# A routed expert kernel: the nest of wide tiles behind the sure tiles, and row scatters that are no longer paced

## The chip, the cores and the metric

The kernel runs on one core of a Trainium2 chip. That core has five engines that run side by side and wait for one another through semaphores: TensorE (PE in the profile; its weight loads are listed as PEld), VectorE (DVE), ScalarE (ACT), GpSimd (POOL) and SyncE (SP). SP issues most loads; GpSimd issues the indirect transfers, whose row addresses come from a table in on-chip memory. All transfers share 16 DMA engines. The metric is the device time of one execution in microseconds; lower is better.

## The reference

Two blocks follow each other. The first is chunked attention: 4 batches, 8 heads, 768 tokens, 64 values a head. Each chunk of 32 queries sees 8 memory keys and the keys from 16 before to 8 behind its chunk.

```python
scores = scale * np.matmul(q_c, k_full.transpose(0, 1, 3, 2))
a = np.exp(scores - np.max(scores, axis=-1, keepdims=True))
a = a / (np.sum(a, axis=-1, keepdims=True) + 1e-09)
out[:, :, c_start:c_end] = np.matmul(a, v_full)
```

The heads are joined to rows of 512 values, 3072 rows in all. The second block sends each row through one of 8 experts, two matrices of 512x1024 and 1024x512. A row may keep the expert of the row before it, so the choice is a recurrence along the sequence.

```python
fresh_e = int(np.argmax(logits[b, s]))
e = fresh_e if s == 0 or local_gate[b, s] < 0.5 else prev_e
h = np.maximum(x[b, s] @ w1[e], 0.0)
out[b, s] = p[e] * (h @ w2[e])      # p: softmax of the logits
```

Everything is in 32-bit floats.

## The kernel before

**Attention.** The 3072 rows are worked in 32 blocks of 96 rows, eight a batch (the loop at L748). Per block PE makes scores (`s_ps`), ACT their exponentials, PE the values (`o_ps`), DVE divides by the sum and writes the block into `x`, and PE turns it (`xt_ps`). PE's order is that of the program text: L654 wraps every matmul and transpose so that the scheduler keeps its place. Other engines' instructions are ordered by a scheduler.

**Routing.** Four blocks make a half of a batch. For each half, a chain planned for later blocks (`plan_at`, L686 to L697) makes logits, picks, the recurrence over the sequence (two scans on DVE), and a row address for each row. Then `route_rows` (L458) computes the addresses and the scale of each row, and `scatter` (L474) sends the rows of one block to `x_dram`, a DRAM buffer with a region per expert: one indirect transfer of 96 rows on GpSimd. `route_rows` sends the first block of the half; the other three follow one attention block later each (L696). `behind` (L396, used in L479) makes each scatter also wait for `paced[0]`, the DVE instruction that last wrote a block of `x` when the scatter was recorded. For the last batch the scatters stand between the matmuls of the first two expert tiles (`MOVE_2` to `MOVE_6` and `MOVES` in `between`, L884 to L890).

**The early plan.** After two of the four batches (`FORE`), a plan is made of five early tiles (`EARLY`): 128 rows of one expert each, out of rows already there. `gathered` (L610) fetches the rows of a tile from `x_dram` by an indirect transfer. It has to wait until the scatters of the batches in question have landed. The five early gathers are planned one an attention block (L741, `early_gathered`, L712). `first_turned` (L731) turns the first tile on PE while attention's last blocks still run.

**Expert tiles.** A tile is 128 rows through one expert: `hidden` (L785) does 64 short matmuls into `h_ps`, with a ReLU on ACT, `rows_turned` (L715) turns the next tile's rows through the single PSUM buffer `g_ps`, and `product` (L801) does 16 long matmuls into `y_ps`; ACT scales, and GpSimd stores the rows to `out` by an indirect transfer (L809). The weights of a tile are eight loads of 512 KB on SP (L636 for `w1`, L639 for `w2`), into pool `wa` (two buffers) or `wb` (one).

Twelve tiles are always run (`SURE`). A late plan (L899) counts what else is left. In front of the ninth sure tile (`BRANCH`, i = 8) a nest of conditions runs further tiles as counted (`maybe_tiles`, L853); in this input eight of them run. In front of the tenth a second nest runs wide tiles (`wide_tiles`, L867): 128 rows plus 64 more of the same expert, so the hidden matmuls have 192 columns, and the last 64 rows have a product of their own (`unit_product`, L815, stored in L829). Three of eight wide tiles run. The first wide tile's weights are loaded into `wa`, the others' into `wb`. Its rows are gathered during tiles i = 6 and 7 and turned in tile i = 8 (`wide_turned`). The last three sure tiles come behind the nest.

A condition that fails jumps over the rest of its nest to a short block that brings the semaphores to where the skipped instructions would have left them, and for that it waits for the engine's own work; these instructions are listed as `_compat.py:109`. After tile i = 9 GpSimd executes one `drain` (L950). At the end all engines read a count (`kept`, L93), and jump over a general version of the kernel that this input doesn't need (L94).

Of the kernel before, what the change touches and what calls it, by code (L numbers as in the profile page):

```python
# [9 lines left out]
I32 = mybir.dt.int32  # L10
ACT = mybir.ActivationFunctionType
ALU = mybir.AluOpType
# [220 lines left out]
def everything(ctx, tc, q, k, v, w_gate, w_local, w1, w2, x_dram, out, ident, back, kept_i):  # L233
# [117 lines left out]
    def values(pt, vt, n, x):  # L351
        for u in range(2):
            o_ps = ops.tile([QB, HP, VW], F32, name="o_ps", tag=f"o_ps{u}")
            for a in range(HP):
                nc.tensor.matmul(o_ps[:, a], lhsT=pt[:, u, a], rhs=vt[:, 2 * a + u], start=True, stop=True)
            rinv = rinvs[:, n, u]
            nc.vector.reciprocal(rinv, o_ps[:, :, DH:VW])
            paced[0] = nc.vector.tensor_tensor(  # L358
                x[:, 0:D].rearrange("p (a u d) -> p u a d", u=2, d=DH)[:, u], o_ps[:, :, 0:DH],
                rinv.to_broadcast([QB, HP, DH]), op=ALU.mult).ins  # L360

    def turned(x, xt):
        xt_ps = xps.tile([P, DK, QB], F32, name="xt_ps", tag="xps")
# [26 lines left out]


    scatters = {b: [] for b in range(B)}

    paced = [None]

    def behind(ins, name):  # L396
        tc.add_manual_dep(ins, name, mybir.DependencyInfo(
            mybir.DependencyClass.Sync, mybir.DependencyReason.DATA), reason="rows written, or one a block")

    def begin_route():  # L400
        return {n: sm.tile([QB, NQB, w], F32, name=n, bufs=2) for n, w in (("lt", E + 1), ("ex", E))}
# [56 lines left out]
    def route_rows(r, b, half, x):  # L458

        j = HALF * half  # L460
        rank, tot, ex = r["rank"], r["tot"], r["ex"][:, j:j + HALF]
        r_ps = xps.tile([QB, HALF, E], F32, name="r_ps", tag="xps")
        for n in range(HALF):
            nc.tensor.transpose(r_ps[:, n], rank[:, QB * (j + n):QB * (j + n) + QB], identity=ident[:E, :E])
        row = sm.tile([QB, HALF], I32, name="row", bufs=2)
        nc.vector.tensor_reduce(row, r_ps, axis=AX.X, op=ALU.max)
        nc.vector.scalar_tensor_tensor(ex, r_ps, 0.0, ex, ALU.is_gt, ALU.mult)
        prob = sm.tile([QB, HALF, 1], F32, name="prob")
        nc.vector.tensor_reduce(prob, ex, axis=AX.X, op=ALU.add)
        nc.vector.tensor_tensor(x[0:QB, j:j + HALF, D:D + 1], prob, tot, op=ALU.mult)  # L470
        r["row"] = row
        scatter(r, b, j, 0)

    def scatter(r, b, j, n):  # L474
        x = xs[b]
        ins = nc.gpsimd.indirect_dma_start(  # L476
            out=x_dram[:, :], out_offset=bass.IndirectOffsetOnAxis(ap=r["row"][:, n:n + 1], axis=0),
            in_=x[0:QB, j + n].bitcast(I32), in_offset=None).ins
        behind(ins, paced[0].name)  # L479

        tc.declare_no_dep(ins, group="scatters", query=mybir.DependencyQuery.ANY_SYNC, reason="rows are unique")
        tc.add_to_no_dep_group("scatters", ins)
        scatters[b].append(ins)

# [123 lines left out]
    def gathered(tiles, i, after, xs=None):  # L610
        _, rows, _ = tiles
        if xs is None:
            xs = gx.tile([P, XW], F32, name="xs")
        ins = nc.gpsimd.indirect_dma_start(
            out=xs.bitcast(I32), out_offset=None, in_=x_dram[:, :],
            in_offset=bass.IndirectOffsetOnAxis(ap=rows[:, i:i + 1], axis=0)).ins
        for a in after:
            for s in scatters[a]:
                behind(ins, s.name)
        tc.add_to_no_dep_group("scatters", ins)  # L620
        return xs

# [21 lines left out]
    def weights(tiles, i, pool):  # L644
        w, pieces = weights_begun(tiles, i, pool)
        for p in pieces:
            p()
        return w
# [34 lines left out]
    def plan_at(at, step, f, *args):  # L683
        at.setdefault(step, []).append(lambda: f(*args))

    for g in range(NB // HALF):  # L686
        b, half = divmod(g, 2)
        n = HALF * g + HALF + 2
        plan_at(first, n, half_logits, g)
        plan_at(after, n, half_turned, g)  # L690
        plan_at(after, n + 1, lambda b=b, half=half: route_picks(routes[b], half))
        plan_at(after, n + 2, lambda b=b, half=half: route_experts(routes[b], half))
        plan_at(after, n + 3, lambda b=b, half=half: route_ranks(routes[b], b, half))
        plan_at(after, n + 3, lambda b=b, half=half: route_places(routes[b], half))
        plan_at(after, n + 4, rows, b, half)
        for j in range(1, HALF):  # L696
            plan_at(after, n + 4 + j, lambda b=b, half=half, j=j: scatter(routes[b], b, HALF * half, j))  # L697

    early = {}

# [8 lines left out]
        early["w"], pieces = zip(*(weights_begun(early["tiles"], i, wa) for i in range(2)))  # L709
        early["pieces"] = [p for ps in pieces for p in ps]  # L710

    def early_gathered(i):  # L712
        early.setdefault("xs", []).append(gathered(early["tiles"], i, range(FORE)))

    def rows_turned(tiles, i, xs, ps=None, xt=None):  # L715
        _, _, past = tiles
# [21 lines left out]
    n = NQB * FORE + HALF + 2  # L738
    plan_at(after, n, plan_begun)
    plan_at(after, n + 1, planned)  # L740
    for i in range(EARLY):  # L741
        plan_at(after, n + 4 + i, early_gathered, i)
    plan_at(after, NB - 3, first_turned)
    for n in range(NB - 8, NB):
        plan_at(after, n, some_pieces, 1)
# [94 lines left out]
    def wide_gathered(j):  # L840
        for t, xs in zip((wide, unit), wide_slots(j)):
            gathered(t, j, range(B), xs)
# [10 lines left out]
    def maybe_tiles(ctx, n_tiles):  # L853
        last = NTILE - SURE - 1
        for j in range(NTILE - SURE):
# [7 lines left out]
                maybe_turned(j + 1)  # L863
            product(ht, w2_sb, rest[:, j % RING], late[2][:, i:i + 1])

    @with_exitstack
    def wide_tiles(ctx, n_wide, w):  # L867
        for j in range(E):
            ctx.enter_context(tc.If(n_wide > j))
            if j + 2 < E:  # L870
                wide_gathered(j + 2)
            w1_sb, w2_sb = weights(wide, j, wb) if j else w
            ht = hidden(wide_xt[j % 2], w1_sb, rows=MORE, ht=wide_ht[j % 2])
            if j + 1 < E:
                wide_turned(j + 1)
            xs, xs_unit = wide_slots(j)
            product(ht, w2_sb, xs, wide[2][:, j:j + 1])
            unit_product(ht, w2_sb, xs_unit, unit[2][:, j:j + 1], wide_y[j % 2])
# [2 lines left out]
    pools = (wa, wa, wb)  # L881

    after.setdefault(NB, []).insert(0, lambda: turn(NB - 1))
    left = [f for n in range(NB, NB + HALF + 6) for f in first.pop(n, []) + after.pop(n, [])]  # L884
    (TURN, MOVE_2, EXPERTS_0, MOVE_3, RANKS_0, PLACES_0, LOGITS, ROWS_0, TURNED, MOVE_4, PICKS, MOVE_5, EXPERTS_1,
     MOVE_6, RANKS_1, PLACES_1, ROWS_1, *MOVES) = left
    between = {0: {0: [MOVE_2], 1: [TURN], 2: [MOVE_3], 3: [LOGITS], 4: [EXPERTS_0], 5: [TURNED],
                   6: [RANKS_0, PLACES_0, PICKS]},
               1: {0: [ROWS_0], 1: [EXPERTS_1, MOVE_4], 2: [RANKS_1, PLACES_1, MOVE_5], 3: [MOVE_6],
                   7: [ROWS_1, *MOVES]}}  # L890

    late = None
    tile_xs, tile_w, done = early["xs"], list(early["w"]), early["done"]
# [1 line left out]
    for i in range(SURE):  # L895
# [16 lines left out]
        if i == BRANCH:  # L912
            _, (n_tiles, n_wide) = nc.values_load_multi_w_load_instructions(
                n_i, min_val=0, max_val=NTILE, skip_runtime_bounds_check_because="counts of tiles")
            nc.tensor.matmul, nc.tensor.transpose = pinned(matmul), pinned(transpose)
            maybe_tiles(n_tiles)

            wide_w = weights(wide, 0, wa)
            tile_w.append(weights(late, i + 1 - EARLY, wa))
        if i == BRANCH + 1:  # L920
            wide_tiles(n_wide, wide_w)
            nc.tensor.matmul, nc.tensor.transpose = matmul, transpose
        if late is not None:
            while len(tile_xs) < min(i + 4, SURE):
                tile_xs.append(gathered(late, len(tile_xs) - EARLY, range(B)))
            while len(tile_w) < min(i + 3, SURE) and (len(tile_w) <= BRANCH or i > BRANCH):
                tile_w.append(weights(late, len(tile_w) - EARLY, pools[len(tile_w) % 3]))
        if BRANCH - 4 <= i < BRANCH - 2:
            with tc.issue_after(stored):
                maybe_gathered(i - (BRANCH - 4))  # L930
        if BRANCH - 2 <= i < BRANCH:
            with tc.issue_after(stored):
                wide_gathered(i - (BRANCH - 2))
        w1_sb, w2_sb = tile_w[i]
        ht = hidden(xt, w1_sb, between.get(i, {}))
        if i == 0:
# [2 lines left out]
            nc.vector.tensor_copy(kept_i, k_ps)  # L939
        if i + 1 < SURE:  # L940
            tiles, at_i = (early["tiles"], i + 1) if i + 1 < EARLY else (late, i + 1 - EARLY)
            ahead = rows_turned(tiles, at_i, tile_xs[i + 1], xt=held_xt[0] if BRANCH <= i + 1 <= BRANCH + 1 else None)
        if i + 1 == BRANCH:
            maybe_turned(0)
        if i == BRANCH:
            wide_turned(0)
        stored = product(ht, w2_sb, tile_xs[i], past)
        if i == SURE - 3:

            tc.keep_in_program_order(nc.gpsimd.drain())  # L950
        xt, past = ahead
        if i == 0:
            nc.tensor.matmul, nc.tensor.transpose = matmul, transpose


# [38 lines left out]
```

## Time and profile before

| | us |
|---|---|
| median of 3 runs | 516.69 |
| the runs | 516.51, 516.69, 518.14 |
| the profiled execution's own time | 518.14 |
| its span in the profile | 516.2 |
| PE busy | 493.4 (96%) |
| POOL busy | 101.0 (20%) |
| attention until the first expert matmul | 0 to 123.3 |
| first nest (eight tiles) ends on PE | 376.0 |
| second nest (three wide tiles) on PE | 393.5 to 459.7 |
| PE's last matmul ends | 510.1 |

The profile shows one execution. A line of a timeline gives start, duration, engine, source line, operation, output and inputs, the count, and in brackets the idle time in front of it with what ended it. Names that end in q are an engine's own queue: branches, semaphore steps and drains, which do not count as busy. A granted clock below 1.00 means that PE's clock was held back; the digits of the PEclk row are tenths of the full clock in 40 equal slices. An indirect transfer's duration on POOL is the making of its descriptors; it lands some microseconds later.

### The profile page before, as it was taken

How to read it: one execution, taken by the hardware profiler on the slowest of the kernel's cores; microseconds unless marked ns; L12 is line 12 of the kernel's file. 1: busy time of each engine (PE TensorE's matmuls, PEld its weight loads, DVE VectorE, ACT ScalarE, POOL GpSimd, SP SyncE). 2: the span in 40 equal slices, each digit the busy share in tenths (PEclk: the TensorE clock that was granted, in tenths of full speed). 3: DMA queues.
4: the chain of work that ended last, by engine and by line, in shares of the span. 5: the costliest groups of instructions: out<-in, count | busy, mean ns of one | idle time of the engine just before them, and what ended most of it. 6: DMA issues, size and time to landing. Idle time of an engine off the chain costs nothing. (4 is left out here: it accounts for less than half of the span.)

```text
span 516.2 us, 9234 instructions
## 1 busy us (share of the span) xinstructions
PE 493.4 (96%) x3474; PEld 378.8 (73%) x3474; DVE 109.5 (21%) x437; ACT 110.9 (21%) x234; POOL 101.0 (20%) x151
## 2 busy tenths in 40 slices
PE   8999999949999999999999999999989999979995
PEld 5988888839678777777777777777777695838772
DVE  2456668634356000001000000000010000000000
ACT  4555555511111111010111111010111111100100
POOL 3002332335043121122111111001102030210000
PEclk9999999966999999999999999999999999997999
DMA  8988888996999999999989999895179925778000
GB/s 299 366 287 245 264 282 247 374 408 208 413 299 356 396 316 360 344 372 354 335 327 325 315 325 336 318 337 204 38 277 414 359 69 187 291 275 324 22 22 24
DMA packets 49377, 146.01 MB, mean 283 GB/s; under 512 B 7258, under 2 KB 11358, under 8 KB 49312
## 3 DMA queue, kind: packets, MB, share of 16 engines
q1 hardware_dynamic: 42240, 123.38, 67.0%
q0 software_dynamic: 6784, 21.30, 11.3%
q8 instruction: 34, 0.56, 0.4%
q10 hardware_dynamic: 288, 0.52, 0.3%
q14 instruction: 31, 0.25, 0.1%
HBM read 132.57 MB, written 13.00 MB: 282 GB/s over the span
## 5 line engine op out<-in xcount | busy, mean ns | idle before, releaser
L654 PEld LDWEIGHTS h_ps<-held_xt,w_sb 128*128 128x128 f32 x704 | 81.6, 194 | 6.6 <-issue 4.9
L654 PE MATMUL h_ps<-held_xt,w_sb 128*128 128x128 f32 x704 | 82.3, 277 | 0.9 <-ACTq _compat.py:109 0.9
L654 PE MATMUL y_ps<-w_sb,ht 128*128 128x512 f32 x176 | 77.5, 593 | 0.0
L809 POOL DMA_INDIRECT out_dram<-y,to x24 | 24.2, 1006 | 257.0 <-ACT y L808 244.4
L804 PE MATMUL y_ps<-w_sb,ht 128*128 128x512 f32 x160 | 70.5, 592 | 0.0
L793 PEld LDWEIGHTS h_ps<-gxt,w_sb 128*128 128x128 f32 x576 | 65.8, 192 | 3.9 <-issue 3.8
L793 PE MATMUL h_ps<-gxt,w_sb 128*128 128x128 f32 x576 | 66.3, 275 | 0.0
L654 PEld LDWEIGHTS y_ps<-w_sb,ht 128*128 128x128 f32 x176 | 32.6, 190 | 36.9 <-issue 36.4
L804 PEld LDWEIGHTS y_ps<-w_sb,ht 128*128 128x128 f32 x160 | 29.5, 190 | 33.0 <-issue 32.8
L796 ACT ACTIVATE ht<-h_ps 128x512 f32<-128x512 f32 x42 | 25.1, 597 | 126.6 <-PE h_ps L793 65.9
L654 PE MATMUL o_ps<-vt,pt 128*96 128x65 f32 x512 | 51.7, 256 | 0.1
L654 PEld LDWEIGHTS o_ps<-vt,pt 128*96 128x96 f32 x512 | 48.7, 172 | 2.9 <-DVE base L446 1.2
L476 POOL DMA_INDIRECT x_dram<-x,row x32 | 31.4, 983 | 82.0 <-DVE x L470 48.9
L722 DVE COPY held_xt<-g_ps 128x512 f32<-128x512 f32 x13 | 9.0, 692 | 158.6 <-PE g_ps L654 144.1
L654 PEld LDWEIGHTS s_ps<-qt,kt 64*128 64x128 f32 x512 | 29.9, 188 | 6.3 <-issue 2.9
L654 PE MATMUL s_ps<-qt,kt 64*128 64x96 f32 x512 | 32.7, 277 | 0.4 <-ACT pt L348 0.4
L654 PEld LDWEIGHTS h_ps<-x,w_sb 128*128 128x128 f32 x192 | 31.2, 190 | 1.2 <-issue 1.2
L654 PE MATMUL h_ps<-x,w_sb 128*128 128x192 f32 x192 | 31.9, 327 | 0.0
L348 ACT ACTIVATE pt<-s_ps,mask_mid 128x256 f32<-128x256 f32 x72 | 28.0, 481 | 7.1 <-PE s_ps L654 6.5
L358 DVE TENSOR_TENSOR x<-o_ps,rinvs 96x256 f32<-96x256 f32 x64 | 26.3, 418 | 1.2
L808 ACT ACTIVATE y<-y_ps,x 128x512 f32<-128x512 f32 x12 | 8.2, 687 | 83.1 <-PE y_ps L654 76.3
L808 ACT ACTIVATE y<-y_ps,xs 128x512 f32<-128x512 f32 x12 | 8.2, 687 | 83.1 <-PE y_ps L804 61.8
(207 smaller groups left out, 353.6 us busy)
## 6 DMA issues: line engine op xcount, KB each, us to landing
w_sb<-in_w_dram SPq DMA_DIRECT2D x192, 512.0 KB, 7.4
vt<-in_v_dram SPq DMA_DIRECT2D x32, 260.0 KB, 4.2
kt<-in_k_dram SPq DMA_DIRECT2D x30, 256.0 KB, 4.6
qt<-in_q_dram SPq DMA_DIRECT2D x32, 192.0 KB, 4.2
kt<-in_k_dram ACTq DMA_DIRECT2D x2, 256.0 KB, 3.6
x_dram<-x,row POOLq DMA_INDIRECT x32, 6.3
out_dram<-y,to POOLq DMA_INDIRECT x24, 7.2
x<-x_dram,rows_late POOLq DMA_INDIRECT x11, 7.2
```

The costliest lines, as they stand in the source:

```text
L348: nc.scalar.activation(pt[:, :, :, c], st[:, :, :, c], ACT.Exp, bias=m[:, g:g + 1], scale=SCALE)
L358: paced[0] = nc.vector.tensor_tensor(x[:, 0:D].rearrange("p (a u d) -> p u a d", u=2, d=DH)[:, u], o_ps[:, :, 0:DH], rinv.to_broadcast([QB ...
L476: ins = nc.gpsimd.indirect_dma_start(out=x_dram[:, :], out_offset=bass.IndirectOffsetOnAxis(ap=r["row"][:, n:n + 1], axis=0), in_=x[0:QB, ...
L654: return lambda *a, **k: tc.keep_in_program_order(f(*a, **k))
L722: nc.vector.tensor_copy(xt[:, :, 0:P], g_ps)
L793: nc.tensor.matmul(h_ps[:, m], lhsT=w1_sb[:, kk, P * (g + m):P * (g + m) + P], rhs=xt[:, kk, 0:rows], start=(kk == 0), stop=(kk == DK - 1))
L796: nc.scalar.activation(ht[:, g:g + many], h_ps, ACT.Relu)
L804: nc.tensor.matmul(y_ps, lhsT=ht[:, m, 0:P], rhs=w2_sb[:, m], start=(m == 0), stop=(m == FK - 1))
L808: nc.scalar.activation(y, y_ps, ACT.Copy, scale=xs[:, D:D + 1])
L809: return nc.gpsimd.indirect_dma_start(out=out, out_offset=bass.IndirectOffsetOnAxis(ap=to, axis=0), in_=y, in_offset=None, bounds_check=NT ...
```

## The change

Two things change together.

First, the pacing goes. `route_rows` sends the four scatters of a half one behind the other, they no longer wait for `paced[0]`, and the five early gathers are issued together, at the block after the plan.

Second, the wide nest moves behind all twelve sure tiles, to the kernel's end. Its first weights go to `wb`, the others' to `wa` with its two buffers; the late sure tiles from the tenth on take `wa`. The first wide gathers are issued during tiles i = 9 and 10, and the first wide rows are turned in tile i = 11. The drain after tile i = 9 goes; in its place GpSimd drains in front of the nest and once in each wide tile, behind the gathers that the tile issues.

```diff
+        for n in range(HALF):
+            ins = nc.gpsimd.indirect_dma_start(
+                out=x_dram[:, :], out_offset=bass.IndirectOffsetOnAxis(ap=row[:, n:n + 1], axis=0),
+                in_=x[0:QB, j + n].bitcast(I32), in_offset=None).ins
...
-        scatter(r, b, j, 0)
-
-    def scatter(r, b, j, n):
...
-        behind(ins, paced[0].name)
...
-        for j in range(1, HALF):
-            plan_at(after, n + 4 + j, lambda b=b, half=half, j=j: scatter(routes[b], b, HALF * half, j))
...
-    def early_gathered(i):
-        early.setdefault("xs", []).append(gathered(early["tiles"], i, range(FORE)))
+    def early_gathered():
+        early["xs"] = [gathered(early["tiles"], i, range(FORE)) for i in range(EARLY)]
...
-    for i in range(EARLY):
-        plan_at(after, n + 4 + i, early_gathered, i)
+    plan_at(after, n + 2, early_gathered)
...
+    def released():
+
+        tc.keep_in_program_order(nc.gpsimd.drain())
...
             if j + 2 < E:
                 wide_gathered(j + 2)
-            w1_sb, w2_sb = weights(wide, j, wb) if j else w
+            released()
+            w1_sb, w2_sb = weights(wide, j, wa) if j else w
...
-            wide_w = weights(wide, 0, wa)
-            tile_w.append(weights(late, i + 1 - EARLY, wa))
-        if i == BRANCH + 1:
-            wide_tiles(n_wide, wide_w)
-            nc.tensor.matmul, nc.tensor.transpose = matmul, transpose
...
-            while len(tile_w) < min(i + 3, SURE) and (len(tile_w) <= BRANCH or i > BRANCH):
-                tile_w.append(weights(late, len(tile_w) - EARLY, pools[len(tile_w) % 3]))
+            while len(tile_w) < min(i + 3, SURE) and (len(tile_w) <= BRANCH or i >= BRANCH):
+                tile_w.append(weights(late, len(tile_w) - EARLY, wa if i >= BRANCH else pools[len(tile_w) % 3]))
+        if i == SURE - 1:
+            wide_w = weights(wide, 0, wb)
...
-        if BRANCH - 2 <= i < BRANCH:
+        if SURE - 3 <= i < SURE - 1:
             with tc.issue_after(stored):
-                wide_gathered(i - (BRANCH - 2))
+                wide_gathered(i - (SURE - 3))
...
-        if i == BRANCH:
+        if i + 1 == SURE:
             wide_turned(0)
...
-        if i == SURE - 3:
-
-            tc.keep_in_program_order(nc.gpsimd.drain())
...
+    released()
+    wide_tiles(n_wide, wide_w)
+    nc.tensor.matmul, nc.tensor.transpose = matmul, transpose
```

## The prediction

> **What bounds the kernel now.** I read the page's slices first: TensorE (PE) is busy in all but two places, so a change can only save time where PE stands idle or runs slow.
>
> ```profile
> PE   8999999949999999999999999999989999979995
> PEclk9999999966999999999999999999999999997999
> ```
>
> Slice 9 (103 to 116 us) is a hole, with a clock of 0.6 around it; slice 37 (464 to 477 us) follows a smaller one. PE's timeline shows the first, and the table of stretches its clock (last three columns: granted clock, DMA share, GB/s).
>
> ```profile
> 105.33 0.50 PE L654 MATMUL xt_ps<-ident,x 96*128 96x96 f32 x4
> 112.79 1.08 PE L654 MATMUL g_ps<-ident,xs 128*128 128x128 f32 x4 [6.96 <-DMA xs<-x_dram,rows_early]
> 123.31 3.00 PE L654 MATMUL h_ps<-held_xt,w_sb 128*128 128x128 f32 x16
> 126.14 0.49 PE L654 MATMUL xt_ps<-ident,x 96*128 96x96 f32 x4
> ...
> 115.00:120.00 5.00, 4.84 (x32) 4.26 (x29) 1.74 (x7) 0.96 (x2) 2.30 (x2) 0.50 0.84 306
> 120.00:125.00 5.00, 5.00 (x30) 5.00 (x29) 3.14 (x21) 0.60 (x2) 2.36 (x5) 0.50 0.31 76
> ```
>
> PE waits 6.96 us for the first gather of tile rows, then works at half clock until about 125.4 us. GpSimd's timeline (POOL) says why the gather is late:
>
> ```profile
> 98.44 0.92 POOL L476 DMA_INDIRECT x_dram<-x,row  x1 [3.49 <-DVE x L470]
> 100.68 0.92 POOL L476 DMA_INDIRECT x_dram<-x,row  x1 [1.32 <-DVE first L412]
> 106.22 0.99 POOL L614 DMA_INDIRECT xs<-x_dram,rows_early  x1 [4.62 <-issue]
> 107.69 0.95 POOL L614 DMA_INDIRECT xs<-x_dram,rows_early  x1 [0.48 <-DMA x_dram<-x,row]
> ```
>
> Two scatters of batch 2 stand ahead of the gather, and both gathers go out only as those have landed. The second hole is the exit from the wide nest:
>
> ```profile
> 456.07 3.67 PE L654 MATMUL yu_ps<-w_sb,x 128*64 128x256 f32 x32
> 463.45 2.26 PE L793 MATMUL h_ps<-held_xt,w_sb 128*128 128x128 f32 x9 [3.71 <-PEq _compat.py:109]
> 466.16 8.20 PE L793 MATMUL h_ps<-held_xt,w_sb 128*128 128x128 f32 x55 [0.45 <-issue]
> 474.20 0.60 PE L719 MATMUL g_ps<-ident,xs 128*128 128x128 f32 x4
> ```
>
> Finally the queue instructions of the exits, of the drain and of the program's end (from the views of single lines; ns min/median/max, first and last start):
>
> ```profile
> _compat.py:109 PEldq COMPARE_BRANCH  x2: 197/2820/5443, 457.4 to 463.1; - x2
> _compat.py:109 POOLq INC_SWDGE_SEM  x2: 1731/1849/1967, 385.2 to 468.0; - x2
> L950 POOLq DRAIN  x1: 8728/8728/8728, 483.0 to 483.0; - x1
> L990 POOLq DRAIN  x3: 46/113/2506, 512.3 to 515.9; - x3
> ```
>
> PE's branch out of the wide nest took 5.4 us, from 457.4, of which its queued matmuls hid only 2.3. POOL pays a semaphore step of 1.7 to 2.0 us per nest exit. The drain took 8.7 us, hidden.
>
> **Scatters and first gathers.** In the built order of the changed kernel the four scatters of a half follow each other, and the five gathers stand directly behind batch 1's, ahead of batch 2's; they wait for DVE's `rows_early` (89.41 + 0.23) and for batch 1's landings. Batch 1's last half starts at 84.33 us. Back to back, scatters start 1.23 us apart (144.27 to 147.95); with the longer 1.38 us ones (93.58), 1.7 apart. So the fourth starts at 88.0 to 89.4. It lands in 3.2 to 4.3 us as those of 84.3 and 86.5 do, or 7.3 as that of 93.58 does: 91.3 to 96.7. A gather landed in 6.6 us under full DMA load (411 GB/s at 105 to 110): 98 to 103.3. PE wants it at 105.83, so the wait goes, with 2.5 to 8 us to spare, and the half clock with it. From 105.83 to the transpose at 126.14 PE now spends 20.31 us. The same work at full clock, start to start: g_ps 0.43 (354.13), lt_ps 0.79 (92.50), o_ps 1.41 and 1.33 (95.24, 98.20), xt_ps twice 0.43, r_ps with its wait 0.64, l_ps 0.48, a quarter of a tile's h_ps 7.14/4 = 1.79. Sum 7.73, so 12.6 us saved. Late next: DVE's `rank` for r_ps, since its 1.00 us scan (106.65) no longer falls into the hole. Queued in DVE's order: scan until 107.65, tile copy 0.69, then 0.7 us of small rows and half of L452's 0.52. I take 0.4 us (bounds 0 and 1.3, the scan plus 0.3). **First part: -12.2** (-11.3 to -12.6).
>
> The rest hides. The bunched scatters move the same bytes; q, k and v loads land in 4.2 to 4.6 us and are issued two pairs (some 13 us) ahead. The weights of tile 0 were issued by 96.3 and landed within 11.8 us, by 108; its first matmul would now start at about 112. Tile 1's landed by about 120 and are wanted at 129. The five gathers and two more scatters brought forward, about 1.7 MB, delay these by 4 us at 410 GB/s; covered. Batch 2's scatters start behind the gathers, near 101 instead of 98.4; their next readers are the late gathers at 165.9. Tile 2's weights, freed with the attention's buffers, shift with PE.
>
> *The Trainium skill (TensorE: Matmul & The Clock Gate, Part 1) states that about 3.4 us of sustained work opens the gate again. The trace shows 0.50 for some 12 us after work resumes at 112.79. By the rule the hole would cost 7.0 + 1.7 = 8.7, and the sum would be about -14; I go by the rows.*
>
> **The nest moved.** Removed from PE's path: the exit's 3.71 us, and tile 9's slow start (463.45 to its product at 474.64 is 11.19, against 7.57 from 361.44 to 369.01): 3.62. Tile 8 no longer turns two sets of rows through one PSUM buffer (384.17 to 386.53, 2.36 against 0.43): 1.93. Added: tile 11 turns the first wide rows, 0.92 (403.90 to 404.82). PE's last matmul ends 7.33 + 1.93 - 0.92 = 8.3 us earlier. The first nest's exit stays as it is (0.87 idle).
>
> But the second exit now stands on the closing path. Today 6.07 us pass from PE's end (510.13) to the span's (516.2): 1.56 to the last issue, 4.51 for landing, drain and closing barrier; the jump to the end runs beneath. Then: 1.34 from PE to the last half store (415.55 to 416.89), its landing (2.4 to 4.1, the first and last stores on L829; I take 3.0, the landing at 511.69, as the DMA is as quiet there), the semaphore step 1.7 to 2.0 (1.9), 0.85 for reading the count and branching (511.46 to 512.3), the closing drain, 1.4 from drain to span's end (514.8 to 516.2). That drain is bounded by 0.05 and 2.5 (the L990 rows); the 2.5 is mostly a landing (512.3 to 514.8, landing at 514.7) that here is past, so 0.5. Sum 9.0 (7.7 to 12.2): 2.9 lost. PE's own exit (a branch of 3.6 to 5.4, then a 3.3 us branch on L94) ends about a microsecond sooner. **Second part: -8.3 + 2.9 = -5.4** (-6.6 to -2.2).
>
> **Loads, gathers, drains.** On SP the loads behind the first exit (376.2) are now tile 9's, then tile 10's, where wide 0's and tile 9's were. The first eight landed by about 392 (3.7 to 8.9 us for w1, 9.7 to 11.1 for w2) and are wanted at 391.4 (w1, landed by 387) and 398.6 (w2). Wide 0's eight follow tile 11's, from about 408, wanted at 435. The wide weights in two buffers need no wait; in one buffer they had none either: 0. The four first wide gathers move on POOL from behind tiles 5 and 6 to behind tiles 8 and 9, wanted some 20 us later: 0. The drain ahead of the nest (8.7, from about 438) holds POOL's branch and wide 2's gathers, issued about 447, landing by 455, wanted at 468. A drain inside the nest waits for two gathers (6.4 us) and holds the row sums and the tile's store. In a wide tile POOL stood idle 13.52 to 14.05 us ahead of that store, so it hides; after the drain ahead of the nest the first wide store may be 1 to 2 us late, with two tiles to make it up.
>
> **Sum.** -12.2 - 5.4 = -17.6. The profiled execution took 518.14 (span 516.2, 1.94 around it): 500.5. The median, 516.69, stands 1.45 lower: 499.1. Part of that 1.45 may lie in the hole that goes; I predict 499.6.
>
> **Rivals.**
> - *The first gather is still late* (scatters slowed beyond 7.3, gathers crowding one another). For it: DMA share 1.0 and 396 GB/s in 95 to 100; against: the spare 2.5 us even on the slow rows. A 3 us wait plus slow clock as at 463 (3.6) gives 506; if the gather waited on batch 2 as now, 511. Chance 0.10.
> - *The end gains little*: a 2.5 us closing drain, 4.1 landing. 502.8 with the first part whole; inside the likeliest case's range.
> - *Slower: the drains in the nest become the bound.* For it: the only drain with many stores behind it took 8.73. POOL's cycle in a wide tile is 22.09 - 14.05 = 8.0 plus the drain; above 14.05 each of three tiles hands on the excess. At 14.05 + 17.6/3 = 20 us the gain is gone; at 24 the time is 529. Against: drains here follow two gathers and two stores, not the whole kernel's. Chance 0.06.
>
> **How the numbers follow.** Likeliest 0.82: 497.5 (516.69 - 19.2) to 504.6 (518.14 - 13.5). About 0.3% (1.6 us) is what a measurement of this kernel can tell from no change. Faster 0.92 (0.82 + 0.10), same 0.02 and slower 0.06 from the drains. Leaving out the late gather and the drains beyond 505, the range is 497 to 505.
>
> **What would show it.** Right: gathers on GpSimd at about 92 to 98 us, no PE idle near 106, clock 1.00 from there; tiles 8 to 11 at 14.45 us steps and the wide ones at 22.1; last matmul about 20.5 us earlier than 510.1; 9 us behind it. Wrong: `xs` still named as PE's releaser; nest drains above 14 us; PE waiting for tile 9's weights; a clock below 1.00 among the late tiles.

## The result, and the profile after

The changed kernel took 500.22 us, the median of four runs (499.53, 499.84, 500.6, and one run of 1012.47 us at full clock that is left out of the ratio, whose cause is not known). The kernel before took 517.04 us beside it. The ratio is 0.967, with a 95% interval of 0.964 to 0.969. In a second group of six runs the ratio was 0.966 (0.962 to 0.970). The forecast was 499.6 us. The profiled execution took 500.6 us, with a span of 498.5.

The page's slices of the changed kernel show that both holes are gone, and the half clock with them (the 7 in the last slice stands behind PE's end):

```profile
PE   8999999999999999999999999999999999999993
PEclk9999999999999999999999999999999999999997
```

PE's timeline and the table of stretches around the first hole (columns of a stretch: window, its length, busy time with the number of instructions for PE, PEld, DVE, ACT and POOL, then the granted clock, DMA share, GB/s):

```profile
106.15 0.50 PE L644 MATMUL xt_ps<-ident,x 96*128 96x96 f32 x4
106.75 0.66 PE L644 MATMUL g_ps<-ident,xs 128*128 128x128 f32 x4
114.55 0.49 PE L644 MATMUL xt_ps<-ident,x 96*128 96x96 f32 x4
...
105.00:110.00 5.00, 4.90 (x53) 3.81 (x52) 4.31 (x12) 1.59 (x4) 0.92 (x1) 1.00 1.04 361
120.00:125.00 5.00, 5.00 (x32) 3.65 (x31) 4.23 (x16) 0.83 (x2) 0.00 (x0) 1.00 1.03 391
```

`g_ps` begins without a wait where it had waited 6.96 us. From the end of the block's `xt_ps` (106.65) to the `xt_ps` inside tile 0 (114.55) PE spends 7.90 us instead of 20.31: 12.41 less. In this profile the stretch itself began 0.82 us later than before. GpSimd's timeline shows what made that possible. The fourth scatter of the half is out at 88.82, the gathers follow from 94.97, and the next batch's scatters stand behind them:

```profile
88.82 0.92 POOL L466 DMA_INDIRECT x_dram<-x,row  x1 [0.31 <-issue]
94.97 0.99 POOL L603 DMA_INDIRECT xs<-x_dram,rows_early  x1 [5.22 <-DMA x_dram<-x,row]
...
101.32 0.94 POOL L466 DMA_INDIRECT x_dram<-x,row  x1 [0.30 <-DVE first L406]
```

The late part, from PE's timeline. The first line is the tile behind the first nest's exit, with the same 0.87 us gap as before; then the first two wide tiles, and the last matmuls of the kernel:

```profile
365.33 7.41 PE L644 MATMUL h_ps<-held_xt,w_sb 128*128 128x128 f32 x64 [0.87 <-ACTq _compat.py:109]
...
423.82 10.56 PE L644 MATMUL h_ps<-x,w_sb 128*128 128x192 f32 x64
445.81 10.67 PE L644 MATMUL h_ps<-x,w_sb 128*128 128x192 f32 x64
...
486.39 3.67 PE L644 MATMUL yu_ps<-w_sb,x 128*64 128x256 f32 x32
```

Before, the last matmuls were these:

```profile
503.10 7.03 PE L804 MATMUL y_ps<-w_sb,ht 128*128 128x512 f32 x16
```

PE's last matmul ends at 490.06 instead of 510.13. The difference of 20.07 is 12.41 from the first stretch, 8.48 from there to PE's end, less the 0.82. Behind PE's end come 8.44 us instead of 6.07. The queue's own instructions (ns min/median/max, then first and last start) and GpSimd's last two stores tell what these consist of:

```profile
L855 POOLq DRAIN  x4: 5359/5893/10461, 425.3 to 470.3; - x4
L976 POOLq DRAIN  x3: 46/107/282, 497.3 to 498.2; - x3
_compat.py:109 POOLq INC_SWDGE_SEM  x2: 213/932/1651, 373.1 to 496.1; - x2
...
487.52 1.02 POOL L796 DMA_INDIRECT out_dram<-y,to  x1 [10.68 <-ACT y L795]
492.25 0.99 POOL L816 DMA_INDIRECT out_dram<-x,to  x1 [3.72 <-DMA out_dram<-y,to]
```

The last half store waits for the landing of the store ahead of it and is issued 2.19 us behind PE's end. The exit's semaphore step takes 0.21 us, the closing drain at most 0.28. That both are so short turned out to be what the drains inside the nest are for.

### The profile page after: what moved, and what is told of

The parts are those of the page before. It is cut to its first block, busy times and chain, and to the rows that moved or that the text cites. A ratio compares the mean times of both kernels' runs of the same rounds, so it can differ in the third digit from the quotient of the medians.

```text
span 498.5 us, 9231 instructions
## 1 busy us (share of the span) xinstructions
PE 485.0 (97%) x3474; PEld 371.5 (75%) x3474; DVE 109.4 (22%) x437; ACT 111.1 (22%) x234; POOL 99.0 (20%) x151
## 5 line engine op out<-in xcount | busy, mean ns | idle before, releaser
L644 PEld LDWEIGHTS h_ps<-held_xt,w_sb 128*128 128x128 f32 x704 | 80.5, 192 | 6.6 <-issue 4.9
L644 PE MATMUL h_ps<-held_xt,w_sb 128*128 128x128 f32 x704 | 81.3, 275 | 0.9 <-ACTq _compat.py:109 0.9
L780 PEld LDWEIGHTS h_ps<-gxt,w_sb 128*128 128x128 f32 x448 | 51.2, 192 | 2.9 <-issue 2.9
L780 PE MATMUL h_ps<-gxt,w_sb 128*128 128x128 f32 x448 | 51.7, 275 | 0.0
L644 PE MATMUL o_ps<-vt,pt 128*96 128x65 f32 x512 | 49.2, 249 | 0.1
L644 PEld LDWEIGHTS o_ps<-vt,pt 128*96 128x96 f32 x512 | 46.2, 165 | 2.2 <-DVE x L358 0.6
L466 POOL DMA_INDIRECT x_dram<-x,row x32 | 29.6, 926 | 73.9 <-DVE x L464 59.0
L710 DVE COPY gxt<-g_ps 128x512 f32<-128x512 f32 x10 | 6.9, 690 | 95.5 <-PE g_ps L707 52.8
```

The costliest lines, as they stand in the source:

```text
L466: ins = nc.gpsimd.indirect_dma_start(out=x_dram[:, :], out_offset=bass.IndirectOffsetOnAxis(ap=row[:, n:n + 1], axis=0), in_=x[0:QB, j + n ...
L644: return lambda *a, **k: tc.keep_in_program_order(f(*a, **k))
L710: nc.vector.tensor_copy(xt[:, :, 0:P], g_ps)
L780: nc.tensor.matmul(h_ps[:, m], lhsT=w1_sb[:, kk, P * (g + m):P * (g + m) + P], rhs=xt[:, kk, 0:rows], start=(kk == 0), stop=(kk == DK - 1))
```

## The experiments

Four runs take the change apart, and compare with the kernel before beside them (517.69 us). Three vary the drains and the end, in one group with the changed kernel. The last four ran in a third group. There three of them took 519 to 533 us instead of some 500, because of attention, which their edits don't touch; for these three only the late stage can be read. The differences are of medians; the ratios have their 95% intervals.

| run | median us | what is compared | difference |
|---|---|---|---|
| first part alone | 504.55 | before, 517.69 | -13.1, ratio 0.975 (0.969 to 0.981) |
| second part alone | 511.89 | before, 517.69 | -5.8, ratio 0.989 (0.983 to 0.995) |
| gathers together, scatters paced | 506.36 | before, 517.69 | -11.3, ratio 0.979 (0.973 to 0.985) |
| scatters unpaced, gathers paced | 521.70 | before, 517.69 | +4.0, ratio 1.006 (1.001 to 1.011) |
| changed kernel again | 500.17 | before, 518.40 | -18.2, ratio 0.966 (0.962 to 0.970) |
| without the drains | 508.37 | changed, 500.17 | +8.2 |
| stores unordered | 499.91 | changed, 500.17 | -0.3 |
| front drain alone | 500.63 | changed, 500.17 | +0.5 |
| before without its drain | 521.36 | before, 517.19 | +4.2, ratio 1.009 (1.006 to 1.013) |

**The first part alone.** The nest stays in the middle; the edits to the scatters and the early gathers are those of the change:

```diff
-        scatter(r, b, j, 0)
+        for n in range(HALF):
+            ins = nc.gpsimd.indirect_dma_start(
...
-    for i in range(EARLY):
-        plan_at(after, n + 4 + i, early_gathered, i)
+    plan_at(after, n + 2, early_gathered)
```

> The kernel before with the first part alone: scatters one behind the other without the wait for a block, and the five early gathers together; the wide nest stays where it was. Theory (the two parts add up, and this one is worth the 12.3 us that the trace of after shows in the stretch from the attention's last xt_ps to tile 0's): 516.9 - 12.3 = about 504.6, no idle PE near 106, clock 1.00 from 105 to 130, and the exit from the wide nest still costs PE about 3.7 us. Rival (the parts overlap, for instance the second part's saving came only because the loads are shifted by the first): below 502 or above 507.

Measured: 504.55 us, 13.1 less than before. There is no wait at `g_ps`, and the clock is 1.00 from 100 to 130 us. The 12.3 us expected lie inside the interval (9.8 to 15.9 us). PE's timeline has `g_ps` and the exit from the wide nest:

```profile
106.74 0.66 PE L644 MATMUL g_ps<-ident,xs 128*128 128x128 f32 x4
...
451.15 1.98 PE L780 MATMUL h_ps<-held_xt,w_sb 128*128 128x128 f32 x9 [3.01 <-PEq _compat.py:109]
```

The profile's span is 13.7 us shorter than before's. That is the 12.41 us of the stretch, less 0.81 because the stretch began later, plus 2.17 at the exit from the wide nest, which this edit leaves alone. There PE waited 3.01 us and took 9.72 to the tile's product, instead of 3.71 and 11.19.

**The second part alone.**

```diff
-        if BRANCH - 2 <= i < BRANCH:
+        if SURE - 3 <= i < SURE - 1:
             with tc.issue_after(stored):
-                wide_gathered(i - (BRANCH - 2))
+                wide_gathered(i - (SURE - 3))
...
+    released()
+    wide_tiles(n_wide, wide_w)
```

> The kernel before with the second part alone: the wide nest at the end, two buffers, the drains; scatters and early gathers paced as before. Theory (8.5 us off PE's path, 2.4 us more behind PE's end): 516.9 - 6.1 = about 510.8, with PE's 7 us wait near 106 and the clock of 0.50 behind it unchanged. Rival (the end pays only together with the first part): 515 or more.

Measured: 511.89 us, 5.8 less. From PE's timeline, the hole and the kernel's last matmuls:

```profile
113.36 1.09 PE L654 MATMUL g_ps<-ident,xs 128*128 128x128 f32 x4 [7.60 <-DMA xs<-x_dram,rows_early]
...
498.22 3.67 PE L654 MATMUL yu_ps<-w_sb,x 128*64 128x256 f32 x32
```

The hole and the half clock are as before. PE ends at 501.89, 8.24 earlier, and the span at 510.4, so 8.5 us lie behind PE's end instead of 6.07. The two parts alone give 13.1 and 5.8, 18.9 together; the changed kernel gave 16.8 and 18.2 in its two groups. They add up within what the measurements can tell, and the exit is one reason why they need not add up exactly: beyond a tile at full clock it cost PE 7.33 us in the profile of before, 5.16 with the first part alone, and 6.12 with the gathers moved alone (next experiment).

**Which half of the first part counts.** In one run only the gathers move, in the other only the scatters lose their pace.

```diff
 # gathers together, scatters as before
...
-    for i in range(EARLY):
-        plan_at(after, n + 4 + i, early_gathered, i)
+    plan_at(after, n + 2, early_gathered)
```

```diff
 # scatters unpaced, gathers as before
-        behind(ins, paced[0].name)
...
-        for j in range(1, HALF):
-            plan_at(after, n + 4 + j, lambda b=b, half=half, j=j: scatter(routes[b], b, HALF * half, j))
```

> The kernel before with the five early gathers together right behind the plan, but the scatters still one a block with their wait. Theory (it is the place of the gathers, not the pace of the scatters, that counts): the first gather waits only for batch 1's last scatter, issued at 93.6 and landing in about 7.3, so it goes out near 101 and lands near 108; PE waits about 2 us instead of 7. If a wait of 2 us brings no half clock, about 506.5; if the half clock comes as after the 7 us wait (17 us at 0.50), about 512 to 514. Rival (the pace matters as much): 514 or more, with the first gather as late as before.

> The kernel before with the scatters unpaced, but the five early gathers still one a block at their old place. Theory (the bunched scatters help only if the gathers stand directly behind batch 1's): all four scatters of batch 2's first half now stand ahead of the first gather, which waits for the landing of the last of them, near 109, and lands near 115; PE waits about 9 to 10 us, and the time is 518 to 521, slower than before. Rival (unpaced scatters land early enough by themselves): the first gather lands before 106 and the time is 504 to 508.

With the gathers moved alone, GpSimd's and PE's timelines have batch 1's last scatter, the first gather, and PE's wait for it:

```profile
94.19 1.37 POOL L476 DMA_INDIRECT x_dram<-x,row  x1 [1.59 <-DVE x L358]
99.61 0.99 POOL L614 DMA_INDIRECT xs<-x_dram,rows_early  x1 [4.05 <-DMA x_dram<-x,row]
...
107.58 0.63 PE L654 MATMUL g_ps<-ident,xs 128*128 128x128 f32 x4 [1.15 <-DMA xs<-x_dram,rows_early]
```

PE waits 1.15 us, the clock stays at 1.00, and 11.3 of the 13.1 us are won. With the scatters unpaced alone, the same three steps:

```profile
101.68 0.92 POOL L466 DMA_INDIRECT x_dram<-x,row  x1 [0.30 <-issue]
110.03 0.99 POOL L603 DMA_INDIRECT xs<-x_dram,rows_early  x1 [7.42 <-issue]
...
116.79 1.08 PE L644 MATMUL g_ps<-ident,xs 128*128 128x128 f32 x4 [11.39 <-DMA xs<-x_dram,rows_early]
```

Now four scatters of batch 2 stand ahead of the gather instead of two, PE waits 11.39 us, and the kernel is slower than before, by 4.0 us in the medians and by 0.6 to 5.7 by the interval (three of its eight runs took 517 to 518 us). What pays is the gathers' place in GpSimd's queue, directly behind the scatters that they need. Unpacing the scatters is worth some 2 us on top of that. In the profiles the wait that goes is 1.15 us of that; the wide nest's exit, which neither edit touches, was 0.96 us dearer with the gathers moved alone. Without the move of the gathers, unpacing does harm.

**What the drains buy.** The changed kernel with `released` doing nothing:

```diff
     def released():
-
-        tc.keep_in_program_order(nc.gpsimd.drain())
+        pass
```

> The changed kernel without any of GpSimd's drains of its own (in front of the nest and inside it). Theory (the drains cost nothing where they stand, and do work ahead that otherwise falls behind PE's end): the exit's semaphore step takes 1.7 to 2.0 us again instead of 0.21, and the closing drain has more to do, up to the 5 to 10 us that the front drain took; 502 to 508. Rival (they are without effect on the time, and the semaphore step was short for another reason): within 0.5 us of the changed kernel.

Measured: 508.37 us, 8.2 more and just above the range expected; it is so in every one of its six runs (507.7 to 509.1, against 498.8 to 500.5). PE's last matmul ends at 488.75, no later than with the drains, but the span at 506.0. Its closing drain and its exit's semaphore step, from the views of single lines:

```profile
L975 POOLq DRAIN  x3: 40/107/7741, 497.4 to 505.7; - x3
_compat.py:109 POOLq INC_SWDGE_SEM  x2: 1651/1839/2027, 371.4 to 494.4; - x2
```

The closing drain grows from 0.28 to 7.74 us, the semaphore step from 0.21 to 2.03; 9.28 in all. The time from PE's end to the span's end grows from 8.79 us in the changed kernel beside it (489.21 to 498.0) to 17.25. The drains cost nothing where they stand, and without them GpSimd does their work behind PE's end.

With the front drain alone:

```diff
             if j + 2 < E:
                 wide_gathered(j + 2)
-            released()
```

> The changed kernel with the drain in front of the nest alone, none inside it. Theory (the front drain takes the many transfers of the whole kernel off the end, the nest's drains only those of one wide tile): the semaphore step at the exit and the closing drain grow by what three wide tiles leave, 1.5 to 4 us; 501.7 to 504. Rival (what the front drain took is all there is): within 0.5 us of the changed kernel.

Measured: 500.63 us (499.67 to 501.53), 0.5 more than the changed kernel, with overlapping runs. The same two lines:

```profile
L975 POOLq DRAIN  x3: 46/107/1117, 496.0 to 497.7; - x3
_compat.py:109 POOLq INC_SWDGE_SEM  x2: 407/1029/1651, 371.0 to 494.6; - x2
```

What three wide tiles leave is 1.12 and 0.41 us: the direction expected, the size not, and too little for these runs to separate from nothing. Nearly all of the 8 us is had by the one drain in front of the nest. Whether the old kernel had the same from its one drain was asked with the kernel before, without it:

```diff
-        if i == SURE - 3:
-
-            tc.keep_in_program_order(nc.gpsimd.drain())
```

> The kernel before without its one drain behind tile i = 9. Theory (a drain done beside PE's work spares the closing drain 7 to 8 us, whatever the order of the tiles): about 8 us slower than before, 525, with the closing drain near 8 to 10 us. Rival (the old order, with a last store every 14 us, leaves the closing drain nothing): within 1 us of before.

Measured: 521.36 us, 4.2 more than before (3.0 to 6.5 by the interval), about half of what was expected. PE's end is where it was (510.08), and the closing drain is this:

```profile
L987 POOLq DRAIN  x3: 40/113/8057, 512.2 to 520.8; - x3
```

It grew from 2.51 us to 8.06, that is by 5.5. The expectation added the whole length of the drain to the end, and forgot that some 2.5 us of it lie beside the landing of the last store, for which the old closing drain waited anyway.

**The end itself.** The last half store was held 0.85 us by the landing ahead of it. Two runs take that wait away. The first takes the order among the stores away, the second (below) changes the order of the two products.

```diff
...
+        tc.declare_no_dep(ins, group="stores", query=mybir.DependencyQuery.ANY_SYNC, reason="rows are unique")
+        tc.add_to_no_dep_group("stores", ins)
```

> The changed kernel with the stores to the output no longer ordered among one another (their rows are unique). Theory (the last half store stood ready 0.85 us before it was issued, held by the landing of the store ahead of it, and all behind it shifts with it): about 0.85 us less than the changed kernel, 499.3. Rival (the landing, the semaphores or the queue of the transfers set the end anyway): within 0.3 us of the changed kernel.

Measured: 499.91 us, 0.3 less than the changed kernel, which is not separable from nothing. The span did get shorter: 496.65 us against 498.1, the medians of six. But the time around the span grew from 1.9 to 3.2 us. The rival came true in the time, and what it is that moved out of the span, no view of the profile shows. A shorter span is not yet a shorter time.

**Three runs that attention spoilt.** The third group held the changed kernel without the front drain, with one buffer for the later wide weights, and with the unit product first:

```diff
 # no front drain
-    released()
     wide_tiles(n_wide, wide_w)
```

```diff
 # later wide weights in the one-buffer pool, the first in the other
-            w1_sb, w2_sb = weights(wide, j, wa) if j else w
+            w1_sb, w2_sb = weights(wide, j, wb) if j else w
...
-            wide_w = weights(wide, 0, wb)
+            wide_w = weights(wide, 0, wa)
```

```diff
 # unit product first
-            product(ht, w2_sb, xs, wide[2][:, j:j + 1])
             unit_product(ht, w2_sb, xs_unit, unit[2][:, j:j + 1], wide_y[j % 2])
+            product(ht, w2_sb, xs, wide[2][:, j:j + 1])
```

> The changed kernel without the drain in front of the nest; the ones inside it stay. Theory (what counts is that some drain runs before PE's last tile is done; which one is indifferent): the first drain in the nest takes over the front one's work, some 10 us instead of 5.3 to 6.1, still beside PE's 22 us tile; 500.2 us, within 0.5 us of the changed kernel. Rival (the first nest drain then holds the first wide tile's store long enough to hold PE): 502 or more.

> The changed kernel with the later wide tiles' weights in the one-buffer pool, as before, and the first's in the two-buffer pool. Theory (the loads of a wide tile are issued long ahead of their use also with one buffer, as in the trace of before): within 0.5 us of the changed kernel. Rival (the second buffer is needed at the end of the kernel, where the tiles before it share the pool): PE waits for weights in the nest, 502 or more.

> The changed kernel with the product of the 64 extra rows ahead of that of the 128 rows in each wide tile, so that the last store follows 7 us behind the one before it and has no landing to wait for. Theory (the 0.85 us that the last store was held are on the closing path): 0.85 us less than the changed kernel, 499.3. Rival (as the run with unordered stores had it: the span gets shorter and the time does not): within 0.4 us of the changed kernel.

Measured: 528.58, 526.95 and 524.82 us, where some 500 was expected of each. No edit explains it: the loss is complete before tile 0 is done. In the one-buffer run the engines have, up to there, the same instructions in the same order as in the changed kernel (the profile records one weight load in another place), and yet tile 0 ends 27 us later (its `k_ps` at 148.49 instead of 121.28). The loss begins at the first bunch of scatters. ACT's, PE's and GpSimd's timelines of the one-buffer run:

```profile
48.11 0.92 POOL L466 DMA_INDIRECT x_dram<-x,row  x1 [0.30 <-issue]
48.59 0.38 PE L644 MATMUL o_ps<-vt,pt 128*96 128x65 f32 x2 [0.31 <-issue]
50.01 1.20 PE L644 MATMUL o_ps<-vt,pt 128*96 128x65 f32 x11 [1.04 <-issue]
50.19 1.20 ACT L348 ACTIVATE pt<-s_ps,mask_mid 128x256 f32<-128x256 f32 x3 [3.11 <-remote]
```

and the same step in the changed kernel beside the drain runs:

```profile
46.83 1.21 ACT L348 ACTIVATE pt<-s_ps,mask_mid 128x256 f32<-128x256 f32 x3 [0.53 <-PE s_ps L644]
47.55 1.57 PE L644 MATMUL o_ps<-vt,pt 128*96 128x65 f32 x16
```

While the fourth scatter of the bunch is being issued, PE stutters through its `o_ps` matmuls, waiting for nothing that the profile shows. ACT stands 3.11 us for a signal that the profile can put down to no engine, and SP's next load is issued at 50.12 instead of 46.76. The clock then falls to 0.50 for 6.8 us; in the run with the unit product first it stays at 1.00 until 108.8, and in the one without the front drain it stands at 0.50 for 34.1 us. The stall comes again with the scatters from 62.46, with those from 78.41 and with the five gathers from 104.30. The same attention, with the same bunches, ran without any of this in the changed kernel (two groups), in the first part alone and the scatters unpaced alone (on the chip of the third group, earlier), and in all three variants of the second group. The paced kernels of the third group, 17 runs of the kernel before and 10 without its drain, took 513 to 524 us, and the profile of the one without its drain has none of these stalls. So attention stalled in this group with bunched scatters and not with paced ones. That the bunches are the cause is not shown: whether those three programs or the chip at that hour brought it out stays open, and so does whether the run of 1012 us belongs to it; the changed kernel and one of the three, side by side on one chip, would tell, and that was not tried. The traces of this group also hold some 11% fewer records of landings (5,422 to 5,502 against 6,114 to 6,125), in the undisturbed kernel too, so the name of what ACT waited for is not to be relied on. That step of the prediction ("the rest hides") held in the result and is not shown to be safe.

The late stage of these runs is not touched by it, and can be read from the profile alone: from the first matmul behind the first nest to the end of the span.

| profiled run | us |
|---|---|
| changed kernel, its two profiles | 133.2 and 133.5 |
| without the front drain | 133.1 |
| later wide weights in one buffer | 133.1 |
| unit product first | 131.3 |

The front drain's work passes to the first drain in the nest, which takes 12.17 us instead of 5.3 to 5.4, still hidden; the second buffer is worth nothing here. The unit product first does shorten the stage by about 2 us, twice what was expected: PE ends at 510.48, and the last store is issued right behind it.

```profile
503.35 7.13 PE L644 MATMUL y_ps<-w_sb,x 128*128 128x512 f32 x16
511.54 0.99 POOL L796 DMA_INDIRECT out_dram<-y,to  x1 [5.70 <-ACTq _compat.py:109]
```

The time around its span was 2.0 us, as with the changed kernel, so here the gain should reach the time, some 498 us where attention runs undisturbed. That version was not measured so, and the number is an estimate from one profile.

## Why the prediction was right

**The first part: predicted -12.2, measured -13.1 alone, and -12.41 in the trace's stretch.** The stretch is what the prediction summed; in the -13.1 a dearer attention (0.81) and a cheaper exit (2.17) are mixed in, so part of that agreement is luck. The terms held: fourth scatter at 88.82 (88.0 to 89.4 predicted), gathers from 94.97 (92 to 98), their landing 6.9 to 8.0 us (6.6). DVE's `rank` delayed nothing that can be seen, where 0.4 was taken. The rival of a late first gather shows in the two halves of the part: 1.15 us of wait with the gathers moved alone, 11.39 with the scatters unpaced alone.

**The Trainium skill's rule against the row.** Before, the clock stood at 0.50 until 125.4 us, 12.6 us behind the return of work at 112.79, and without the hole the stretch took 12.41 us less. The run of the first part alone gained 9.8 to 15.9, which the rows' 12.2 fits. By the Trainium skill, "TensorE: Matmul & The Clock Gate", Part 1, some 3.4 us of sustained work opens the gate again, and by that the hole would have cost an estimated 8.7 us. These runs don't fit that.

**The nest: predicted -8.3 on PE, measured -8.24 alone.** The steps of 14.45 and 22.1 us came as said, and the first exit kept its 0.87. The 7.33 us for the second exit are those of one profile; the other profiles with the nest in the middle have 5.16 to 7.59.

**Behind PE's end: predicted +2.9, measured +2.4, with the right sum by luck, out of wrong terms.** Four terms were mis-sized. The last half store was put 1.34 us behind PE's end and came at 2.19, as the landing of the store ahead of it was left out. Its landing was put at 3.0 us and took 3.7; the bounds of 2.4 and 4.1 left out the middle store of the three on L829, which took 6.4. Against that, the semaphore step was put at 1.9, from exits with no drain close ahead of them, and took 0.21; and the closing drain was put at 0.5 and took 0.28.

**The drains: predicted to cost nothing, which held; what they save was not asked.** They are hidden, as worked out, and the first wide store, feared 1 to 2 us late, was not held: the front drain took 10.46 us with GpSimd idle, as this timeline of the changed kernel's GpSimd shows (the gathers behind it, the next store with 0.65 us to spare, and the store after that with the full slack back).

```profile
425.56 0.99 POOL L796 DMA_INDIRECT out_dram<-y,to  x1 [14.02 <-ACT y L795]
436.63 0.99 POOL L603 DMA_INDIRECT x<-x_dram,rows_wide  x1 [10.08 <-issue]
443.61 1.02 POOL L796 DMA_INDIRECT out_dram<-y,to  x1 [0.65 <-ACT y L795]
...
465.42 1.02 POOL L796 DMA_INDIRECT out_dram<-y,to  x1 [10.75 <-ACT y L795]
```

But the prediction priced them only as a cost. It bounded the closing drain by 0.05 and 2.5 us, from a kernel that had itself drained shortly before its end. Without the drains it is 7.74, and by these numbers the nest at the end, without them, would have gained nothing: 5.8 us less 8.2. The slower rival, drains that become the bound, was far off: 5.4 to 5.9 us in the nest, where more than 14 would have been needed to hold PE, and about 20 to lose the gain.

**Weights, gathers and loads at nothing:** no wait of PE for weights in the late part, and the stage with one buffer is as long as with two.

## What to carry to other kernels

Here GpSimd's first gather went out only behind the scatters that stood ahead of it, whether it needed them or not (PE waited 1.15 us with no scatter too many ahead, 11.39 with four). So place the transfer that someone waits for directly behind those that it truly needs, before taking any pace out of the others. GpSimd's drain was cheaper a little before the end, beside work of other engines, than behind it (by 8.2 us here and 4.2 in the kernel before): what a drain costs is read where it stands, what it saves is read at the end of the kernel. And a run whose loss lies in a stage that the edit does not touch answers nothing about the edit as a whole; its other stages can still be read.

## What the runs showed of the hardware that was not expected

**The half clock comes in steps of 3.41 us, mostly more of them behind a longer wait.** Its length, from windows of 0.1 us, against the wait that brought it:

| PE's wait | half clock |
|---|---|
| 0.87 and 1.15 us | none |
| 2.77, 2.83, 3.35 and 3.71 us (exit of the wide nest: gathers moved alone, scatters unpaced alone, before without its drain, before) | 6.83 us, twice 3.41 |
| 3.01 us (the same exit, first part alone) | 3.41 us, once |
| 6.96, 7.13 and 7.60 us (first hole: before, before without its drain, second part alone) | 17.07 us, five times |
| 11.39 us (first hole: scatters unpaced alone) | 23.9 us, seven times |

At the exits a second, shorter wait of 0.45 to 1.72 us follows the first. In the last row it begins 2.1 us into the wait and ends 14.6 us behind it (the clock is the third number from the end):

```profile
107.50:107.60 0.10, 0.00 (x0) 0.00 (x0) 0.00 (x0) 0.00 (x0) 0.00 (x0) 0.51 0.76 246
...
131.30:131.40 0.10, 0.10 (x2) 0.10 (x2) 0.00 (x0) 0.00 (x0) 0.00 (x0) 0.53 0.83 205
131.40:131.50 0.10, 0.10 (x3) 0.10 (x2) 0.00 (x0) 0.00 (x0) 0.00 (x0) 1.00 1.23 328
```

The Trainium skill, "TensorE: Matmul & The Clock Gate", Part 1, names a window of about 3.4 us, with which the step agrees. By the same part one busy window is enough to open the gate. In these runs the clock came back 3.8 us behind the return of work once (first part alone, 451.15 to 454.9), and 6.2 to 14.6 us behind it in the other eight cases of the table. The wait's length is not a sharp rule either: in the one-buffer run a stutter with two waits of 0.31 and 1.04 us was followed by 6.8 us of half clock, and in the profile without the front drain one with waits of 0.35 and 0.50 us by 34.1 us, ten steps, with PE at work nearly all the time.

**The kernel before has two levels by itself.** Of 39 runs of it beside the experiments most took 516 to 519 us at a mean clock of 0.973 to 0.978, and eight took 513 to 514 at 0.981 to 0.988: part of the half clock is not always there. The changed kernel, the first part alone and the gathers moved alone, without the long wait, have a mean clock of 0.99 or more. So have the variants of the second group, but for the kernel without the drains (0.986 to 0.987), whose PE stands idle for 17 us at the end.
